# Attention scores on half of TensorE's rows per head, two units at a time, with q and k turned by one DMA

## The chip, the cores and the metric

The kernel runs on one core of a Trainium2 chip. The metric is the device time of one execution in microseconds. A run is called slow only if it is over 1.5% above the fastest run of the same kernel; every time compared here is of fast runs unless a sentence says otherwise. Five engines work beside each other: TensorE (PE, with its weight loads PEld), VectorE (DVE), ScalarE (ACT), GpSimd (POOL) and SyncE (SP), which here issues DMA.

## The reference, cut to what matters

```python
# q, k, v: [4 batches, 8 heads, 768 tokens, 64]; is_retrieval = [1,0,1,0,0,0,1,0]
scores = q @ k.T / sqrt(64)
keep   = causal if retrieval head else causal & (key < 4 or q - key < 64)
a      = softmax(where(keep, scores, -1e9))
x      = (a @ v) -> [3072 tokens, 512]
h      = x @ w_in                     # [3072, 2048]
out    = (h - tanh(h)) @ w_out        # [3072, 512]
```

## The kernel before

The 3072 tokens are cut into 12 tiles of 256 tokens (NG = 3 to a batch, NB = 2 blocks of 128 tokens in each). The eight heads form four pairs; one pair in one tile is a *unit*. Tiles 0 to 2 treat all heads alike. From tile 3 on the heads are sorted by their retrieval flag ("ranked"), so that half of the units need only the keys near the query. A planner written into the kernel orders all instructions beforehand; it lays score units, attention-value products (`av`), the first dense layer (`ph`) and the second (`po`) between each other on TensorE.

A head has only 64 elements, and the array has 128 rows. The kernel before fills all rows all the same: a 128-row tile of q holds both heads of a pair, and k of each head is stored with the other head's 64 rows set to zero.

```python
GROUPS = {                      # (key block, first query block, query blocks)
    0: [[(0, 0, 2), (1, 1, 1)]],
    1: [[(2, 0, 2), (3, 1, 1), (1, 0, 1)], [(1, 1, 1), (0, 0, 2)]],
    2: [[(4, 0, 2), (5, 1, 1), (3, 0, 1)], [(3, 1, 1), (0, 0, 2)], [(1, 0, 2), (2, 0, 2)]],
}
def st_S(n, gi):                # one group of one unit
    ...
        for hh in range(2):     # head 0 first, then head 1
            o = 0
            for jb, q0, nb in grp:
                nc.tensor.matmul(
                    out=sc()[:, hh, o : o + nb * 128],
                    lhsT=kk[:, hh, jb * KS : jb * KS + 128],           # 128 rows, 64 of them zeros
                    rhs=q_of(t, hp)[:, q0 * 128 : (q0 + nb) * 128], ...)
                o += nb * 128
    ...   # exp on ScalarE into pt, mask on VectorE
```

Ranked tiles are gathered, cast to fp16 on GpSimd one head at a time, and turned by SyncE's DMA transposes, q and k apart:

```python
def cast_ranked(t):
    ...                                         # zero the padding of k once per buffer
    for half in range(2):
        for nm in "kqv":
            for rank in range(half * HH, half * HH + HH):
                ...  # nc.gpsimd.tensor_copy(out=..., in_=r()[:, :, at, :])   24 casts a tile
    for nm in "kq":
        for i in range(NB):                     # 4 transposes a tile
            ...
                if nm == "k": o, src = kz[b % 2][:, :, c0 : c0 + 128], kp          # 8 blocks
                else:         o, src = qT[t]()[:, :, i * 128 : ...], t16s["q", t]() # 4 blocks
                nc.sync.dma_start_transpose(out=o, in_=src[:, i, :, :]...)
```

The softmax here doesn't subtract the row's maximum and nothing guards it: scores larger than these inputs give would overflow.

## Time and profile before

| | before |
|---|---|
| time, median of 3 runs | 250.95 us (250.09 to 251.23) |
| span of the profiled run | 249.8 us |
| PE / DVE / ACT / POOL busy | 231.0 / 147.0 / 146.9 / 100.5 us |
| score matmuls | 412, with 70,656 columns |
| DMA packets | 120,133 |

The first part of the page gives the busy time of each engine, its share of the span, and its instructions:

```profile
PE 231.0 (92%) x2220; PEld 176.1 (70%) x2220; DVE 147.0 (59%) x363; ACT 146.9 (59%) x225; POOL 100.5 (40%) x288
```

PE is far ahead of the others. But a busy share is an average over a start in which PE waits for loads, a weak stretch between 50 and 77 us, and a long stretch in which it never rests; the prediction takes them apart. One more view is SyncE's timeline (start, length, engine, line, operation) around the first ranked tile:

```profile
60.25 2.73 SPq L714 DMA_TRANSPOSE kz<-k  x2
63.16 2.50 SPq L714 DMA_TRANSPOSE qT<-t_q  x2
```

The reader is to see two transposes of k, with 8 blocks of 128 columns each, and two of q, with half as many blocks. The first ranked scores come in PE's timeline after the last of them:

```profile
68.30 0.49 PE L1000 MATMUL sc<-qT,kz 128*128 128x256 f16 x4
```

### The profile page before, as it was taken

Reading aid. Unit: us, or ns where it says so; the run is one execution under the profiler, and the core shown is the slowest. Engines: PE = TensorE matmul, PEld = TensorE weight load, DVE = VectorE, ACT = ScalarE, POOL = GpSimd, SP = SyncE. Lnnn points to the kernel's source line nnn. Section 1 sums busy time; section 2 is a strip of 40 time slices with the busy share of each in tenths; the row PEclk is TensorE's granted clock in tenths of the full one; section 3 lists DMA queues with packets and bytes.
Section 4 is the critical chain, followed back from the end, with each engine's and each line's share of the span. In section 5 each row is a group of like instructions: output and inputs, shape, how many; then the busy total and the mean of one; then the engine's idle time right before and its main releaser. Section 6 shows DMA issues by size and latency. Waiting matters only on the chain. (4 is left out here: it accounts for less than half of the span.)

```text
span 249.8 us, 6122 instructions
## 1 busy us (share of the span) xinstructions
PE 231.0 (92%) x2220; PEld 176.1 (70%) x2220; DVE 147.0 (59%) x363; ACT 146.9 (59%) x225; POOL 100.5 (40%) x288
## 2 busy tenths in 40 slices
PE   1788989989969999999999999999999999999992
PEld 0466978757657689877777777777877777777751
DVE  7555854495397486857946655467676554643410
ACT  3578855487462677864567575647567566443330
POOL 5386260009997443946716359265340000000000
PEclk9999999999988999999999999999999999999997
DMA  6999999996799899959979999999962211031111
GB/s 137 220 189 206 214 211 133 206 219 115 172 242 148 178 162 201 187 128 267 192 181 194 172 228 179 228 185 174 217 133 87 59 42 43 3 87 45 42 69 63
DMA packets 120133, 38.47 MB, mean 154 GB/s; under 512 B 114338, under 2 KB 116642, under 8 KB 120098
## 3 DMA queue, kind: packets, MB, share of 16 engines
q1 hardware_dynamic: 110882, 32.91, 67.4%
q0 software_dynamic: 8928, 4.98, 14.4%
q8 instruction: 18, 0.29, 0.5%
q10 hardware_dynamic: 288, 0.14, 0.2%
q14 instruction: 17, 0.14, 0.2%
HBM read 27.27 MB, written 6.29 MB: 134 GB/s over the span
## 5 line engine op out<-in xcount | busy, mean ns | idle before, releaser
L1172 PE MATMUL ph<-xT,win 128*128 128x256 f16 x768 | 101.1, 274 | 1.0 <-DVE gt L1192 0.8
L1231 PE MATMUL po<-wout,gt 128*128 128x512 f16 (+1 forms) x400 | 98.7, 373 | 0.3 <-ACT ot L1207 0.2
L1192 DVE SCALAR_TENSOR_TENSOR gt<-th,ph 128x512 f16<-128x512 f32 x96 | 65.6, 684 | 49.9 <-ACT th L1185 49.8
L1185 ACT ACTIVATE th<-ph 128x512 f32<-128x512 f32 x96 | 57.3, 599 | 60.1 <-PE ph L1172 58.5
L1172 PEld LDWEIGHTS <-win 128*128 128x128 f16 x768 | 81.2, 114 | 10.6 <-issue 1.9
L1018 ACT ACTIVATE pt<-sc 128x768 f16<-128x768 f32 (+1 forms) x60 | 54.0, 917 | 12.4 <-PE sc L1000 12.1
L1231 PEld LDWEIGHTS <-gt 128*128 128x128 f16 x400 | 37.3, 98 | 24.1 <-DVE gt L1192 0.8
L697 POOL CAST k<-raw_k 128x128 f16 x72 | 19.7, 309 | 45.5 <-DMA raw_k<-in_k_dram 27.6
L1067 PEld LDWEIGHTS <-pt 128*128 128x128 f16 x552 | 26.2, 98 | 11.7 <-DVE pt L1031 2.3
L1000 PE MATMUL sc<-qT,kz 128*128 128x256 f16 (+1 forms) x280 | 32.8, 251 | 1.3 <-DMA qT<-t_q 0.7
L1000 PEld LDWEIGHTS <-kz 128*128 128x128 f16 x280 | 23.3, 99 | 9.2 <-issue 2.2
L1067 PE MATMUL av<-v,pt 128*128 128x65 f16 x304 | 25.7, 195 | 2.0 <-DVE pt L1031 2.0
L697 POOL CAST v<-raw_v 128x128 f16 x72 | 21.7, 341 | 9.1 <-DMA raw_v<-in_v_dram 9.1
L697 POOL CAST t_q<-raw_q 128x128 f16 x72 | 21.7, 330 | 7.0 <-DMA raw_q<-in_q_dram 6.6
L1097 DVE TENSOR_TENSOR x16t<-av,rinv 128x128 f32 x72 | 20.8, 289 | 2.0
L1067 PE MATMUL av<-vf,pt 128*128 128x65 f16 x248 | 20.4, 193 | 1.4 <-ACT pt L1018 0.9
L1207 ACT ACTIVATE ot<-po 128x512 f32<-128x512 f32 (+1 forms) x24 | 14.2, 590 | 12.0 <-PE po L1231 9.6
L943 ACT ACTIVATE pt<-sc 128x1024 f16<-128x1024 f32 (+1 forms) x18 | 17.2, 955 | 6.0 <-PE sc L929 4.6
L1087 DVE RECIPROCAL rinv<-av 128x4 f32<-128x4 f32 x48 | 8.6, 179 | 13.9 <-PE av L1067 13.4
L1036 DVE TENSOR_TENSOR pt<-pt,m 128x1024 f16<-128x1024 f16 x16 | 11.8, 735 | 8.3 <-ACT pt L1018 8.2
L960 DVE TENSOR_TENSOR pt<-pt,mS 128x512 f16<-128x512 f16 x24 | 10.0, 456 | 7.3 <-ACT pt L943 7.3
L929 PE MATMUL sc<-qT,kz 128*128 128x128 f16 x132 | 10.4, 220 | 0.0
(73 smaller groups left out, 127.2 us busy)
## 6 DMA issues: line engine op xcount, KB each, us to landing
out_dram<-ot SPq DMA_DIRECT2D x23, 256.0 KB, 2.4
raw_q<-in_q_dram SPq DMA_DIRECT2D x18, 256.0 KB, 4.8
raw_k<-in_k_dram SPq DMA_DIRECT2D x18, 256.0 KB, 4.4
raw_v<-in_v_dram SPq DMA_DIRECT2D x18, 256.0 KB, 4.6
win<-in_moe_w_in_dram POOLq DMA_DIRECT2D x4, 512.0 KB, 8.8
wout<-in_moe_w_out_dram POOLq DMA_DIRECT2D x4, 512.0 KB, 15.9
raw_q<-in_q_dram SPq DMA_DIRECT2D x8, 128.0 KB, 3.8
raw_k<-in_k_dram SPq DMA_DIRECT2D x8, 128.0 KB, 3.8
```

What stands on the lines that cost most here:

```text
L697: nc.gpsimd.tensor_copy(out=o, in_=r()[:, :, at, :])
L943: lambda: nc.scalar.activation(out=pt()[:, :, 0:wid], in_=sc()[:, :, 0:wid], func=AF.Exp, scale=inv_sqrt_d),
L1000: nc.tensor.matmul(out=sc()[:, hh, o : o + nb * 128], lhsT=kk[:, hh, jb * KS : jb * KS + 128], rhs=q_of(t, hp)[:, q0 * 128 : (q0 + nb) * 128],
L1018: lambda: nc.scalar.activation(out=pt()[:, :, 512 * gi : 512 * gi + wid], in_=sc()[:, :, 0:wid], func=AF.Exp, scale=inv_sqrt_d,),
L1036: nc.vector.tensor_mul(out=pv, in0=pv, in1=m4[:, hs, 256:512].unsqueeze(2).to_broadcast([128, 2, 2, 256]),)
L1067: nc.tensor.matmul(out=av()[:, i, hh, :], lhsT=pt()[:, hh, co : co + 128], rhs=vv, start=(jb == first_jb), stop=(jb == qb),)
L1097: nc.vector.tensor_mul(out=x16s[t]()[:, :, at, :], in0=av()[:, :, hh : hh + 1, 0:D], in1=rinv()[:, :, hh : hh + 1].unsqueeze(3).to_broadca ...
L1172: nc.tensor.matmul(out=ph()[:, j, :], lhsT=w()[:, cb, c0 + fb % 4 : c0 + 512 : 4], rhs=xTs[t]()[:, cb, :], start=(cb == 0), stop=(cb == HP ...
L1185: lambda: nc.scalar.activation(out=th()[:], in_=ph()[:], func=AF.Tanh, scale=1.0 / XS),
L1192: lambda: nc.vector.scalar_tensor_tensor(out=gts[t]()[:, u * FU : (u + 1) * FU, :], in0=th()[:], scalar=-XS, in1=ph()[:], op0=ALU.mult, op ...
L1207: nc.scalar.activation(out=ot()[:, c0:c1], in_=po()[:, c0:c1], func=AF.Copy, scale=1.0 / XS)
L1231: nc.tensor.matmul(out=po()[:, c0:c1], lhsT=gts[t]()[:, f, ts * 128 : ts * 128 + 128], rhs=w_out_t[f // 4]()[:, f % 4, c0:c1], start=(f == ...
```

## The change

The intent is to let the two heads of a pair work at the same time, one on rows 0 to 63 and one on rows 64 to 127 of the array. Then no zeros are needed. Score groups of two units are put behind each other, so that TensorE changes between 128-row and 64-row work less often. And since k is no longer wider than q, both lie in one tile, are cast in one instruction per head, and are turned in one transpose per block.

```diff
-    kz = [const.tile([128, H, 2 * NG * KS], FP16, name=f"kz{s}") for s in range(2)]
-    k16 = [const.tile([128, NB, H, 128], FP16, name=f"k16_{x}") for x in range(2)]
+    qk = [const.tile([128, 2 * HP, 2 * NG, KS], FP16, name=f"qk{s}") for s in range(2)]
+    t16 = [const.tile([128, NB, 2, H, D], FP16, name=f"t16_{x}") for x in range(2)]
 ... (zero_kz and its eight calls go, and so does the memset of k16)
-                for nm in "kqv":
+                for nm in ("qk", "v"):
 ...
+                                nc.gpsimd.tensor_copy(
+                                    out=t16[t % 2][:, :, :, rank : rank + 1, :],
+                                    in_=raws["rqk", t][0]()[:, :, :, at, :],
+                                )
 ...
-            for nm in "kq":
-                for i in range(NB):
 ...
+            for i in range(NB):
+                def turn(i=i):
+                    nc.sync.dma_start_transpose(
+                        out=qk[b % 2][:, :, g * NB + i, 0:128],
+                        in_=t16[t % 2][:, i].rearrange("p x h d -> p (x h d)"),
+                    )
 ...
-        def st_S(n, gi):
+        def st_S(*units):
 ...
+                for n, gi, grp, wid, sc, key, added in todo:
+                    for jb, c0, i, nb in grp:
+                        for hh in range(2):
+                            p_ = slice(64 * hh, 64 * hh + 64)
+                            nc.tensor.matmul(
+                                out=sc()[:, hh, o : o + nb * 128]...,
+                                lhsT=ks...[p_, jb * KS + c0 : jb * KS + c0 + 128],
+                                rhs=qs[p_, q0 + i : q0 + i + nb, 0:128], ...
+                            )
 ...
+            two = 1 if todo[0][0] // HP in (0,) else 2
+            clusters.setdefault(todo[0][0], []).append(todo[:two])
```

## The prediction

> **What bounds the kernel now.** I began with the table of stretches (busy time of each engine, granted clock, DMA share), cut where the character of the run changes.
>
> ```profile
> 0.00:23.00 23.00, 14.20 (x125) 9.16 (x126) 14.50 (x52) 14.46 (x25) 13.88 (x31) 1.00 1.10 186
> 23.00:50.00 27.00, 26.15 (x252) 21.73 (x251) 14.94 (x32) 16.24 (x30) 6.93 (x8) 1.00 1.28 192
> 50.00:77.00 27.00, 23.56 (x257) 16.82 (x255) 18.45 (x54) 17.92 (x26) 20.23 (x59) 0.94 0.97 183
> 77.00:245.00 168.00, 166.97 (x1596) 128.35 (x1592) 98.71 (x226) 98.26 (x146) 59.50 (x190) 1.00 0.72 142
> 245.00:250.00 5.00, 0.15 (x2) 0.00 (x0) 0.42 (x1) 0.00 (x0) 0.00 (x0) 0.73 0.13 40
> ```
>
> The columns are the length, then PE, PEld, DVE, ACT and POOL busy, then clock, DMA share and GB/s. From 77 to 245 us PE is busy 166.97 of 168 us, and no other engine is above 98.71: TensorE is the bound there, and in 23 to 50 us (26.15 of 27). Two stretches are different. Before 23 us PE works 14.20 us and waits for first loads and casts. In 50 to 77 us it stands 3.4 us, and the clock drops. The page's groups say what the scores cost:
>
> ```profile
> L1018 ACT ACTIVATE pt<-sc 128x768 f16<-128x768 f32 (+1 forms) x60 | 54.0, 917 | 12.4 <-PE sc L1000 12.1
> L697 POOL CAST k<-raw_k 128x128 f16 x72 | 19.7, 309 | 45.5 <-DMA raw_k<-in_k_dram 27.6
> ...
> L1000 PE MATMUL sc<-qT,kz 128*128 128x256 f16 (+1 forms) x280 | 32.8, 251 | 1.3 <-DMA qT<-t_q 0.7
> ...
> L929 PE MATMUL sc<-qT,kz 128*128 128x128 f16 x132 | 10.4, 220 | 0.0
> ```
>
> The busy time of a matmul includes its tail, which lies beside the next one, so I take the pace from starts in PE's timeline:
>
> ```profile
> 48.04 0.94 PE L1000 MATMUL sc<-qT,kz 128*128 128x256 f16 x10
> 48.81 0.60 PE L1172 MATMUL ph<-xT,win 128*128 128x256 f16 x4
> ...
> 70.20 0.60 PE L1172 MATMUL ph<-xT,win 128*128 128x256 f16 x4
> 72.82 0.36 PE L1067 MATMUL av<-v,pt 128*128 128x65 f16 x6 [2.02 <-DVE pt L1031]
> 73.02 0.61 PE L929 MATMUL sc<-qT,kz 128*128 128x128 f16 x6
> 73.42 1.06 PE L1231 MATMUL po<-wout,gt 128*128 128x512 f16 x2
> ```
>
> Ten score matmuls hold 1792 columns (1024 of one group, 768 of the other) and take 48.81 - 48.04 = 0.77 us: 0.43 ns a column. The kernel has 140 score matmuls of 256 columns and 272 of 128: 70,656 columns, 30.4 us of PE's stream. Half of the rows of each are multiplied by zeros. The last lines show the hole: 2.02 us of waiting, then two 512-column matmuls in 0.86 us (73.42 to the next start, 74.28) where 0.43 is usual, thus at half clock. DVE's timeline has its origin:
>
> ```profile
> 69.73 3.03 DVE L1031 TENSOR_TENSOR pt<-pt,m 128x768 f16<-128x768 f16 x1 [0.35 <-ACT pt L1018]
> 72.68 0.64 DVE L953 TENSOR_TENSOR pt<-pt,mS 128x768 f16<-128x768 f16 x1
> 73.25 0.68 DVE L1192 SCALAR_TENSOR_TENSOR gt<-th,ph 128x512 f16<-128x512 f32 x1
> 73.84 0.17 DVE L1087 RECIPROCAL rinv<-av 128x4 f32<-128x4 f32 x1
> 73.94 0.54 DVE L1031 TENSOR_TENSOR pt<-pt,m 128x768 f16<-128x768 f16 x1
> ```
>
> The same mask takes 3.03 us once and 0.54 us four microseconds later; meanwhile POOL runs casts without a pause.
>
> **What the Trainium skill says.** (1) "TensorEngine Tiling (Array Packing)", Key Properties: tiles run independently, but changing the mode drains TensorE; its Gotcha 1 wants different row tiles in different PSUM banks. No matmul before uses fewer than 128 rows, so this trace can neither agree nor disagree; the diff does put the two heads in separate 512-float halves. (2) "TensorE: Matmul & The Clock Gate", Part 3: tiles of different rows overlap, four of 32 rows gave 3.07 times; Part 2 puts the drain of the array at about 128 cycles, 53 ns at 2.4 GHz. Here a lone tail can be read: a 128-column matmul is busy 220 ns and streams 128 x 0.43 = 55, so 165 ns of latency follow it. (3) The same page, Part 1: after an idle window the clock halves for about 3.4 us. The trace agrees: half pace from about 73 to 77 us after the 2.02 us hole. (4) "GPSIMD Engine Reference", Key points: GpSimd shares SBUF interfaces with VectorE, contending with two-input VectorE instructions. The 3.03 us mask agrees.
>
> **The change part by part.** The order of the built kernel shows the same 412 score matmuls, each on 64 rows, heads alternating, in 41 unbroken runs (before: 69): four single units in the first tile, then 37 pairs of groups. The other PE counts are unchanged.
>
> *Scores.* If two heads truly overlap, 30.4 us become 15.2. What lies before 23 us is worth little, since PE waits there anyway: 6,656 columns and 6 runs. After 23 us there remain 64,000 columns, 27.5 us, half of which is 13.8 us saved. A 128-column pair needs two weight loads in 55 ns; 65-column matmuls start every 30 ns with a load each, so two loads are about 60 ns. This lengthens the 136 such pairs by some 5 ns, 0.7 us; I leave it inside the next figure.
>
> *Mode changes.* 35 runs after 23 us mean 70 changes. The floor is the 53 ns of (2). The ceiling is the whole 165 ns tail and then a bare weight load (98 ns on the page), 263 ns. In between, the array drains and one load is laid bare: 53 + 98 = 151 ns, less whatever overlaps. I choose 125 ns: 70 x 0.125 = 8.8 us. That the author pairs units at all says that a change isn't free. Net on the path: 13.8 - 8.8 = **5.0 us**.
>
> *First ranked tile (50 to 77 us).* POOL now casts q and k of a head in one instruction: 216 casts become 144, of which 72 have twice the size. From 0.31 us for 128 elements and 0.62 for 512, one of 256 is estimated at 0.41, so 72 x (0.41 + 0.34) = 54 us in place of 63; the zero memsets of k (2 x 0.52 us) go and the sink copies halve. Per tile, all q and k casts end about 1.7 us earlier, and the transposes, four issues from 60.25 to 65.66 us in SyncE's timeline, become two, 8 blocks of 128 columns in place of 12. The first ranked scores can thus start some 2 to 3 us sooner. The hole costs 2.0 us and the half clock half of 3.4, 1.7: 3.7 us. Whether a mask meets a train of casts again is chance, so I count 60%: **2.2 us**.
>
> *Start.* VectorE loses the eight zero memsets (1.02 to 4.28 us) and half of the k copies (30 to 18 in all, 0.29 us each). The first score waited 0.45 us for a k copy; after that the loads rule: **0.3 us**.
>
> *Cost.* A pair fills both score buffers at once, so it waits for both earlier exponentials, and two follow in a row on ACT (0.8 to 1.0 us each), ahead of a tanh that frees a hidden-layer bank. ACT is at 59% and PE has other matmuls to run, so I put down only **0.8 us** of new waits.
>
> *Beside the path.* DMA moves a third fewer transpose blocks, DVE 3.0 + 3.5 us less, POOL some 12 us less. From 77 us on none of that is what PE waits for: worth nothing by itself.
>
> Sum: 250.95 - 5.0 - 2.2 - 0.3 + 0.8 = **244.25 us**.
>
> **Rivals.** *Changes cost the ceiling.* 70 x 0.263 = 18.4 us against 13.8: PE loses 4.6, and the time is 250.95 + 4.6 - 1.7 = 254. For it speaks the 165 ns tail; against it that the array's own part of the tail is only a third and that the change was built around few runs. *Changes are nearly free.* At the floor they cost 3.7 us, PE gains 10.1, and the time is about 239. For it: PE pulls weight loads ahead, which hides them everywhere in this trace. *The two heads don't overlap* (the same feeding path, or loads that serialise): the 13.8 us vanish and some 8.8 are added: 258 or so. Only the skill's 3.07 of four speaks against it. *Another bound takes over.* In 23 to 50 us the DMA share is 1.28 and POOL waits 27.6 us for k; a faster PE asks for data sooner. But from 77 us on the share is 0.72, transposes shrink, and SyncE loads two tiles ahead. If the pairing stalls PE more than I think (2 to 3 us), the time ends at 246 to 247.
>
> **Range and chances.** The cost of a change dominates: every 25 ns move the end by 1.75 us. 75 to 180 ns spans 240.7 to 248.1; the hole adds about 2 us either way. I give 238.5 to 249.5. The limit of 2% is 245.9; my centre is 1.7 us below it, about half of my spread: faster by over 2% with 0.62, within 2% with 0.31, slower by over 2% with 0.07.
>
> **What would show it.** In the changed profile, starts of the two matmuls of a head pair should lie within some 10 ns, and a run of 1792 columns should last about 0.385 us plus two changes. From the last 128-row start to the first 64-row start beyond the stream's own time I expect 100 to 150 ns, and the same on the way back. PE should still be about 99% busy from 77 us to some 238. The hole near 70 us should be smaller and the half clock gone or short. If the starts don't pair, the halving is wrong; if gaps exceed 190 ns, the cost of changes is; if PE shows waits for exponentials or score buffers over 1 us in all after 77 us, pairing has become a bound of its own; waits for the transposed q and k there would mean that DMA has.

## The result, and the profile after

The changed kernel took 241.63 us (median of 4 runs, 240.8 to 243.5), the kernel before 251.09 us in the same rounds (250.09 to 252.69). A ratio in this document is the mean time of one kernel's fast runs over that of the other's of the same rounds, so it is not quite the ratio of the medians quoted. Here it is 0.963, with a 95% interval of 0.955 to 0.970. The profiled run of the changed kernel, with a span of 239.1 us, was the fastest of its four; a second trace of the same kernel, taken later as a control, has 241.3 us.

The first part of the page after, and the table of stretches (length; PE, PEld, DVE, ACT, POOL busy; clock; DMA share; GB/s), cut at the same times:

```profile
PE 221.2 (93%) x2220; PEld 158.0 (66%) x2220; DVE 138.3 (58%) x343; ACT 144.8 (61%) x225; POOL 87.6 (37%) x214
```

```profile
0.00:23.00 23.00, 14.16 (x137) 8.86 (x138) 11.20 (x40) 14.94 (x26) 13.92 (x31) 1.00 1.10 187
23.00:50.00 27.00, 25.25 (x253) 19.34 (x251) 15.53 (x41) 17.45 (x31) 6.44 (x7) 1.00 1.35 202
50.00:77.00 27.00, 25.43 (x323) 17.62 (x322) 18.13 (x55) 19.83 (x29) 18.87 (x49) 1.00 0.95 210
77.00:234.00 157.00, 156.08 (x1513) 112.10 (x1512) 93.01 (x210) 92.61 (x141) 48.33 (x128) 1.00 0.63 130
```

PE is still the bound in the long stretch (156.08 of 157 us), and that stretch is some 11 us shorter. Between 50 and 77 us PE is busier (25.43 us in place of 23.56), does 323 matmuls where it did 257, and the clock no longer drops. Between 23 and 50 us it is a little less busy than before. The groups of the page that answer to those of before:

```profile
L906 ACT ACTIVATE pt<-sc 128x1024 f16<-128x1024 f32 (+1 forms) x78 | 68.2, 925 | 9.3 <-PE sc L886 8.1
L630 POOL CAST t<-raw_rqk 128x256 f16 x72 | 27.7, 427 | 58.8 <-DMA raw_rqk<-in_k_dram 42.6
...
L886 PE MATMUL sc<-qk 64*128 64x128 f16 (+1 forms) x412 | 23.0, 239 | 1.5 <-DVE qk L776 1.2
L886 PEld LDWEIGHTS <-qk 64*128 64x128 f16 x412 | 13.7, 95 | 12.6 <-issue 8.9
```

All 412 score matmuls are `64*128` now. The cast of q and k together took 427 ns (the prediction put 410). The pace is read from starts, as before:

```profile
119.62 1.03 PE L1139 MATMUL po<-wout,gt 128*128 128x512 f16 x4
120.58 0.62 PE L886 MATMUL sc<-qk 64*128 64x128 f16 x14
121.13 0.20 PE L975 MATMUL av<-vf,pt 128*128 128x65 f16 x1
...
123.31 1.04 PE L1080 MATMUL ph<-xT,win 128*128 128x256 f16 x8
124.28 0.56 PE L886 MATMUL sc<-qk 64*128 64x128 f16 x12
124.77 1.04 PE L1139 MATMUL po<-wout,gt 128*128 128x512 f16 x4
```

The 14 matmuls of the first run hold 2048 columns and last 121.13 - 120.58 = 0.55 us. On 128 rows at 0.43 ns a column they would have taken 0.88. The cost of the change is in the same lines: eight `ph` matmuls of 256 columns stream for 0.87 us, but the next start comes after 0.97 (124.28 - 123.31). Those 0.1 us are the way into the 64-row mode.

I took the whole trace apart in this way. The *stream* is each matmul's columns at 2.4 columns a nanosecond (0.417 ns each) plus 2.5 ns (fitted to the starts of back-to-back matmuls in these traces, which lie 56 ns apart for 128 columns, 109 for 256 and 216 for 512), halved where two heads work as a pair. A *change* is what lies beyond the stream at the edges of a 64-row run (counted up to 0.10 us going in and 0.11 going out). *Waits* are all the rest of the time between two starts, half clock included. From first to last start of a matmul, in us:

| kernel | stream | changes | waits to 23 us | 23-50 | 50-77 | after 77 | sum |
|---|---|---|---|---|---|---|---|
| before | 220.5 | 0 | 9.2 | 1.0 | 6.1 | 2.5 | 239.3 |
| after | 205.3 | 8.3 | 7.5 | 2.8 | 2.4 | 2.2 | 228.5 |
| after, second trace | 205.3 | 8.3 | 8.6 | 2.6 | 2.4 | 3.6 | 230.7 |

So 15.2 us of stream went, 8.3 came back as changes, and waits fell by 3.9 us in the one trace and by 1.6 in the other. The median of a change over the runs is 95 ns going in and 106 ns coming out. The two starts of a head pair lie 3 to 4 ns apart.

The hole near 70 us has gone. VectorE's timeline shows the mask of the first ranked tile:

```profile
64.64 0.73 DVE L936 TENSOR_TENSOR pt<-pt,m 128x768 f16<-128x768 f16 x1
65.29 0.75 DVE L924 TENSOR_TENSOR pt<-pt,mS 128x768 f16<-128x768 f16 x1
...
66.27 0.56 DVE L936 TENSOR_TENSOR pt<-pt,m 128x768 f16<-128x768 f16 x1
```

It takes 0.73 us, where the same mask took 3.03 before, although GpSimd casts the next tile beside it here too (62.84 to 66.30 us). Its scores start earlier (62.76 us, before 68.30), and so does what they rest on. First GpSimd's first casts of q and k before, then those after, then SyncE's transposes and PE's first ranked scores after:

```profile
55.88 0.29 POOL L697 CAST k<-raw_k 128x128 f16 x1 [17.91 <-DVE pt L1036]
```

```profile
53.66 2.48 POOL L630 CAST t<-raw_rqk 128x256 f16 x7 [16.03 <-DVE qk L776]
```

```profile
56.75 2.75 SPq L648 DMA_TRANSPOSE qk<-t  x2
```

```profile
62.76 0.51 PE L886 MATMUL sc<-qk 64*128 64x256 f16 x10
```

The casts start 2.2 us earlier. The transposes are through at 59.50 us (56.75 + 2.75), where the four of before were through at 65.66 (63.16 + 2.50).

### The profile page after: what moved, and what is told of

It is laid out like the page before. It is cut to its first block, busy times and chain, and to the rows that moved or that the text cites. A ratio compares the mean times of both kernels' runs of the same rounds, so it can differ in the third digit from the quotient of the medians.

```text
span 239.1 us, 5924 instructions
## 1 busy us (share of the span) xinstructions
PE 221.2 (93%) x2220; PEld 158.0 (66%) x2220; DVE 138.3 (58%) x343; ACT 144.8 (61%) x225; POOL 87.6 (37%) x214
## 5 line engine op out<-in xcount | busy, mean ns | idle before, releaser
L1080 PEld LDWEIGHTS <-win 128*128 128x128 f16 x768 | 80.0, 114 | 14.1 <-issue 3.0
L906 ACT ACTIVATE pt<-sc 128x1024 f16<-128x1024 f32 (+1 forms) x78 | 68.2, 925 | 9.3 <-PE sc L886 8.1
L630 POOL CAST t<-raw_rqk 128x256 f16 x72 | 27.7, 427 | 58.8 <-DMA raw_rqk<-in_k_dram 42.6
L625 POOL CAST v<-raw_rv 128x128 f16 x72 | 22.5, 353 | 6.1 <-DMA raw_rv<-in_v_dram 6.1
L886 PE MATMUL sc<-qk 64*128 64x128 f16 (+1 forms) x412 | 23.0, 239 | 1.5 <-DVE qk L776 1.2
L886 PEld LDWEIGHTS <-qk 64*128 64x128 f16 x412 | 13.7, 95 | 12.6 <-issue 8.9
L931 DVE TENSOR_TENSOR pt<-pt,mS 128x512 f16<-128x512 f16 x24 | 11.1, 503 | 6.6 <-ACT pt L906 6.6
L793 PEld LDWEIGHTS <-t 128*128 128x128 f16 x48 | 4.2, 109 | 9.2 <-ACT t L594 5.7
L701 POOL TENSOR_TENSOR vf<-v,rflagr 128x260 f16<-128x260 f16 x12 | 7.3, 615 | 0.0
L471 DVE TENSOR_SCALAR m<-A,thr 128x512 f16<-128x512 f16 x16 | 5.9, 418 | 2.0 <-PE sc L873 1.6
```

What stands on the lines that cost most here:

```text
L625: nc.gpsimd.tensor_copy(out=v1s[b]()[:, lo : lo + NB, rank : rank + 1, 0:D], in_=raw_of("v", t)[:, :, at, :],)
L630: nc.gpsimd.tensor_copy(out=t16[t % 2][:, :, :, rank : rank + 1, :], in_=raws["rqk", t][0]()[:, :, :, at, :],)
L886: nc.tensor.matmul(out=sc()[:, hh, o : o + nb * 128].rearrange("p (i c) -> p i c", c=128), lhsT=ks.rearrange("p i c -> p (i c)")[p_, jb * ...
L906: lambda pt=pt, gi=gi, wid=wid, sc=sc: nc.scalar.activation(out=pt()[:, :, 512 * gi : 512 * gi + wid], in_=sc()[:, :, 0:wid], func=AF.Exp, ...
L1080: nc.tensor.matmul(out=ph()[:, j, :], lhsT=w()[:, cb, c0 + fb % 4 : c0 + 512 : 4], rhs=xTs[t]()[:, cb, :], start=(cb == 0), stop=(cb == HP ...
```

## The experiments

Three theories stood after the result. *Rows*: the gain is the two heads at once, less what the changes of mode cost. *Hole*: a good part is that the first ranked tile comes sooner, for which casts, transposes or zeros could be the reason. *Pairing*: the order of matmuls inside a run, or the pairing of units, matters by itself. Eleven kernels were run. All passed the comparison with the reference; two of them (e4, e8) compute wrong scores, and pass all the same, probably because q and k of standard deviation 0.1 make scores so small that the softmax hardly feels them. The kernel before took 251.83 us (e1 to e4) and 252.5 on another chip. So the ratios are compared, not the times.

### e1: one unit at a time

```diff
-            two = 1 if todo[0][0] // HP in (0,) else 2
+            two = 1
```

> The changed kernel with every score unit alone: 70 runs of half-row matmuls in place of 41, nothing else. Theory (a run costs some 0.2 us of mode changes, 0.095 in and 0.106 out as in the changed kernel's trace, and all of it is on the path): 29 x 0.2 = 5.8 us more, 247.4 us. Rival 1 (pairing stalls PE on the score buffers, singles are smoother): 240 us or less. Rival 2 (a change is hidden, pairing is worth nothing): 241 to 242 us.

It took 248.14 us, ratio 0.985 (0.980 to 0.990). With 70 runs of scores in place of 41 the changes sum to 14.2 us in place of 8.3. That is 5.9 us more, and the time is 248.14 us against 243.16 in the control, 5.0 us apart (by the ratios, 0.985 against 0.965 and 0.963, it is 4.9 to 5.5 us). Up to 1.7 us of this may be something else: all four runs of e1 show a granted clock of 0.988 to 0.991, and in its trace the clock is halved from 21.3 to 24.7 us, which neither trace of the changed kernel shows. A change costs the same as in the paired kernel (96 ns and 106 ns). In PE's timeline a run of eight matmuls takes 0.33 us (125.23 - 124.90), of which 0.11 is the way out; the way in, another 0.1, lies before its start (the eight `ph` stream for 0.87 us and take 0.97):

```profile
123.93 1.04 PE L1080 MATMUL ph<-xT,win 128*128 128x256 f16 x8
124.90 0.40 PE L886 MATMUL sc<-qk 64*128 64x128 f16 x8
125.23 1.04 PE L1139 MATMUL po<-wout,gt 128*128 128x512 f16 x4
```

Changes are thus on the path, and their number is what pairing units is for.

### e2: head 0's matmuls first, then head 1's

```diff
-                    o = 0
-                    for jb, c0, i, nb in grp:
-                        for hh in range(2):
-                            p_ = slice(64 * hh, 64 * hh + 64)
+                    for hh in range(2):
+                        p_ = slice(64 * hh, 64 * hh + 64)
+                        o = 0
+                        for jb, c0, i, nb in grp:
```

> The changed kernel with the loops swapped: in each group first all matmuls of head 0, then all of head 1, so that neighbours use the same rows and can't overlap except at a seam. Mode changes stay at 41 runs. Theory (the gain comes from two row tiles streaming at once): the score stream goes back from 15.2 to nearly 30.4 us, of which 13.6 lie after 23 us, less a seam of some 0.1 us for each of 78 groups: +6 to +13 us, 248 to 255 us. Rival (PE looks ahead and overlaps them anyway, or the gain has another source): 241 to 243 us.

The loss that I expected did not come: 242.9 us, ratio 0.967 (0.961 to 0.973), the same as the changed kernel.

```profile
120.83 1.03 PE L1139 MATMUL po<-wout,gt 128*128 128x512 f16 x4
121.78 0.63 PE L886 MATMUL sc<-qk 64*128 64x128 f16 x14
122.34 0.20 PE L975 MATMUL av<-vf,pt 128*128 128x65 f16 x1
```

The run of 14 matmuls (2048 columns) takes 0.56 us although in the program all of head 0's matmuls of a group stand before head 1's. One after the other they would need 2048 x 0.417 = 0.85 us for the stream alone. The single starts in the trace show how. The second group of this run is, in program order, 256, 128, 128 columns of head 0 and then 256, 128, 128 of head 1; by start it is

```
122.019 (256 columns)  122.032 (256)  122.128 (128)  122.141 (128)  122.184 (128)  122.197 (128)
```

The second 256-column matmul, head 1's first, starts 13 ns after the first and ahead of two matmuls that precede it in the program. (In the built program, PE's instructions stand in the program's order, so it was not the compiler that moved them.) TensorE thus finds the other head's work by itself, within the two or three matmuls that stood between here. Alternating the heads in the program is not what earns the time.

### e3: the kernel before, with half rows alone

```diff
-                for hh in range(2):
-                    o = 0
-                    for jb, q0, nb in grp:
+                o = 0
+                for jb, q0, nb in grp:
+                    for hh in range(2):
+                        p_ = slice(64 * hh, 64 * hh + 64)
-                            lhsT=kk[:, hh, jb * KS : jb * KS + 128],
-                            rhs=q_of(t, hp)[:, q0 * 128 : (q0 + nb) * 128],
+                            lhsT=kk[p_, hh, jb * KS : jb * KS + 128],
+                            rhs=q_of(t, hp)[p_, q0 * 128 : (q0 + nb) * 128],
 ... (the same for the near units, and the planner's cost of a score group set to fit)
```

> The kernel before, with zeros, separate transposes and its own order, but each score matmul on its head's 64 rows and the heads alternating: 69 runs. Theory: 13.6 us of stream saved after 23 us, some 60 runs there x 0.2 us = 12 us given back: about 1.5 us faster than before, 249.5 us, if the hole near 70 us stays as it is (246 if it closes). Rival (the halving alone makes the whole gain): 241 to 242 us.

It took 251.52 us, ratio 0.9995 (0.994 to 1.005): no gain at all. The stream is shorter by the same 15.2 us, but the 69 runs of the old order cost 14.0 us of changes. The little that is left, 1.2 us, is lost in waits. The table of waits has PE wait for DMA, in us in total, times, and the longest:

```profile
PE sc L1003 <- DMA qT<-t_q: 2.9, 4, 0.9
...
PE ph L1175 <- DMA xT<-x16t: 1.3, 2, 1.0
```

Before, the first of these was 0.7 us and the second absent. After 77 us the waits are 7.1 us, before 2.5. So halving the rows pays here only with fewer runs. The waits for SyncE's queue can't come from a faster PE here, since stream and changes together are only 1.2 us shorter than before. PE comes earlier all the same, because the hole near 70 us is missing (waits up to 77 us are 13.2 us, before 16.3), although this kernel has the casts, the transposes and the zeros of before. Its first ranked mask runs in the middle of a train of casts, and takes 0.64 us:

```profile
69.15 0.64 DVE L1034 TENSOR_TENSOR pt<-pt,m 128x768 f16<-128x768 f16 x1 [0.30 <-ACT pt L1021]
69.33 1.48 POOL L697 CAST v<-raw_v 128x128 f16 x3
```

### e4: the changed kernel on all rows

```diff
-                            p_ = slice(64 * hh, 64 * hh + 64)
+                            p_ = slice(0, 128)
 ... (and the planner's cost of a score group set to that of before)
```

The result is wrong: both heads' products are added in each head's scores.

> The changed kernel with all 128 rows in each score matmul (so that the two heads' scores are added: a wrong result on purpose), no mode changes, everything else of the change kept. Theory: 13.6 us of stream come back after 23 us and 7.1 us of mode changes go: +6.5 us, 248.1 us, which leaves some 3 us of the gain to the other parts (the hole near 70 us). Rival (the other parts are worth nothing): 251 us, as before.

It took 246.82 us, ratio 0.981 (0.976 to 0.987). So everything but the rows is worth 251.83 - 246.82 = 5.0 us; I had put 3 here, and 2.5 less the cost of pairing in the prediction. The rest of the ratio, from 0.981 to the changed kernel's 0.965 or 0.963, is what the rows are worth net of their changes: 4.0 to 4.6 us, where the prediction had 5.0. Stream and changes together are 6.9 us shorter (15.2 - 8.3), so more than 2 us of that were met by new waits. The stream is that of before (220.5 us) and there are no changes of mode; waits are 13.2 us in place of 18.8. The half clock is gone, and the waits between 50 and 77 us fall from 6.1 to 1.6 us. The table of stretches shows this at full rows and with 25.92 us of busy PE:

```profile
50.00:77.00 27.00, 25.92 (x303) 19.84 (x301) 17.17 (x57) 19.17 (x28) 17.45 (x45) 1.00 0.92 206
```

### e5: the kernel before, with one tile's casts held back

The casts of tile 4 wait for a value of the first ranked tile's exponentials, so that GpSimd is idle while VectorE masks.

```diff
+                held = op("POOL", 100,
+                    lambda: nc.gpsimd.tensor_copy(out=gate2[:], in_=pts[n]()[0:1, 0, 0:1]), ...)
-                            port=True,
+                            port=True, after=held,
 ... (a memset of k is held too, and the casts of tile 4 are planned one unit later)
```

> The kernel before with one edit: GpSimd's casts for tile 4 wait (by a one-element copy that reads the masked tile) until the first two masks of tile 3 are done. Theory (the hole near 70 us is a mask held up by GpSimd's train of casts, and the half clock follows from it): the mask takes 0.55 us in place of 3.03, the 2.0 us wait and the half clock go, about 3 us faster than before, 248 us. Rival (the hole has another cause, such as too little work for PE there): 250 to 252 us with the wait still there under another name.

```profile
69.97 0.56 DVE L1040 TENSOR_TENSOR pt<-pt,m 128x768 f16<-128x768 f16 x1 [0.35 <-ACT pt L1027]
```

The mask that took 3.03 us takes 0.56 without casts beside it, and the waits between 50 and 77 us fall from 6.1 to 3.2 us. That fits the theory, but it doesn't settle it. Casts beside a mask are not enough to stretch it so: the same mask beside casts took 0.64 us in e3 and 0.73 in the changed kernel. In the thirteen kept traces some 200 masks have casts beside them for more than 0.7 of their time, and after the 3.03 us the longest took 0.92. So the 3.03 us is a rare event in the one trace that was kept of the kernel before; what sets it off stays open.

The half clock behind it was not usual either. It lasts 3.4 us, which takes 0.007 from the mean granted clock of a run of 250 us (the profiled run has 0.988). Of 19 runs of the kernel before, 14 have 0.996 or more and so can't have had it, and they are no faster (250.76 to 254.32 us) than the other five (251.26 to 253.07). The hole is thus a poor measure of what the change could gain.

As a test of what the hole is worth the run failed: it took 254.67 us, ratio 1.009 (1.005 to 1.012). The held casts run from 71.4 to 80 us in place of 66.7 to 75, the transposes behind them come late, and waits after 77 us rise to 7.8 us, part of it a half clock of 3.4 us from 97.7.

### e6 and e9: q and k turned apart again

e6 put two transposes into each planned step, but let the planner count one:

```diff
-                    nc.sync.dma_start_transpose(
-                        out=qk[b % 2][:, :, g * NB + i, 0:128],
-                        in_=t16[t % 2][:, i].rearrange("p x h d -> p (x h d)"),
-                    )
+                    for x in range(2):
+                        nc.sync.dma_start_transpose(
+                            out=qk[b % 2][:, x * HP : (x + 1) * HP, g * NB + i, 0:128],
+                            in_=t16[t % 2][:, i, x].rearrange("p h d -> p (h d)"),
+                        )
```

> The changed kernel with two crossbar transposes for a block, one for q and one for k, in place of one: same data, 18 more issues. Theory (not on the path; the queue of SyncE has room): within 0.5 us of the changed kernel, 241 to 242.2 us. Rival (the transposes pace the ranked tiles): 2 us or more slower, 243.5 us or above, with PE waiting on transposes.

It took 257.92 us, ratio 1.022 (1.017 to 1.026), 16 us above what I expected. Its table of waits has one line with three stands of up to 4.5 us, and its clock was halved four times (at 18.3, 76.3, 120.7 and 178.7 us):

```profile
PE ph L1081 <- DMA xT<-x16t: 9.4, 3, 4.5
```

The planner had counted too little for SyncE, so the size says nothing fair about the change. e9 therefore gives each transpose a planned step of its own and its own key:

```diff
-                op(
-                    "SP", 1250, turn, ...
-                    w=[("qk", b % 2, "all", g, i)], dma=(1024, 22.0),
-                )
+                for x, nm in ((1, "k"), (0, "q")):
+                    ...
+                    op(
+                        "SP", 1250, turn, ...
+                        w=[("qk", b % 2, nm + "all", g, i)], dma=(512, 22.0),
+                    )
```

> The changed kernel with separate transposes for q and k again, this time as operations of their own, so that the planner counts each issue on SyncE's queue (in the earlier run it counted one for two). Theory A (each transpose holds SyncE's queue some 1.3 us whatever its size; with PE faster the queue paces the ranked tiles): still 4 us or more slower than the changed kernel, above 246 us, PE waiting on the transposes of x and of q and k. Theory B (the earlier loss came from the planner's false count alone): 241 to 243.5 us.

It took 248.6 us, the median of its three fast runs (245.85 to 249.33; the fourth, 249.84, counts as slow), ratio 0.981 (0.974 to 0.989). The changed kernel's ratio in the same rounds was 0.965, so about 1.6% of the time, some 4 us, is lost by this alone. SyncE's timeline shows why:

```profile
57.25 5.63 SPq L650 DMA_TRANSPOSE qk<-t  x4
68.01 6.99 SPq L650 DMA_TRANSPOSE qk<-t  x4
```

Four transposes of 4 blocks each hold the queue for 5.6 to 7.0 us, where two of 8 blocks took 2.75 for the same bytes. What the queue is charged for is the transpose, not its size: the median of all is 1.30 us with 8 blocks (changed kernel) and 1.27 with 4 (e9). PE then waits for q and k, and for the turned x of the dense layer, which goes through the same queue:

```profile
PE sc L888 <- DMA qk<-t: 3.8, 3, 1.6
PE ph L1082 <- DMA xT<-x16t: 2.0, 1, 2.0
```

A half clock of 3.4 us follows the stand of 2.0 us. In the first trace of the changed kernel there is 0.9 us for x (2.3 in the second) and none for q and k:

```profile
PE ph L1080 <- DMA xT<-x16t: 0.9, 1, 0.9
```

### e7: the zeros put back

Eight memsets of the old size go into a tile that nobody reads, at the place where the old ones stood.

```diff
+            for c0, c1 in ((0, TT), (TT, S)):
+                for hp in range(HP):
+                    op("DVE", (c1 - c0) * 1.06 + 20,
+                        lambda hp=hp, c0=c0, c1=c1: nc.vector.memset(spare[:]..., 0.0), w=["spare"])
```

> The changed kernel with the eight zero memsets of the kernel before put back at the start of VectorE's work, on a tile that nobody reads. Theory (the loads rule the start; what the zeros cost is the 0.3 us of the prediction): 241.6 to 242.2 us. Rival (VectorE's 3.3 us stood on the path to the first scores): 243.5 to 245 us.

It took 243.42 us, the median of its five fast runs (241.86 to 245.31; the sixth, 245.61, counts as slow), ratio 0.966 (0.961 to 0.971). The changed kernel has 0.965 in its five-round control. The zeros at the start cost nothing that can be measured here.

### The control: the changed kernel again

> The changed kernel unedited, as the control of this group: a ratio of 0.963 to the kernel before, 241 to 243 us.

It took 243.16 us (242.38 to 245.06), ratio 0.965 (0.961 to 0.969). In its trace one wait for the turned x at 113 us takes 1.6 us, which the first trace does not have. That is the larger part of the difference between the two traces.

### e8: both heads on the same 64 rows

```diff
-                            p_ = slice(64 * hh, 64 * hh + 64)
+                            p_ = slice(0, 64)
 ... (and the planner's cost set to fit)
```

The result is wrong: head 1's scores are head 0's. All else, the 64-row mode, the runs and the transposes, is that of the changed kernel; only the second row half is not used.

> The changed kernel with both heads of a pair on the same 64 rows (rows 0 to 63; a wrong result on purpose): the same 41 runs and mode changes, but no second row tile that could run beside the first. It replaces the loop swap, which showed that PE pairs the tiles whatever their order. Theory (the whole gain of the scores is two row tiles at once): the score stream goes back to 30.4 us, 13.6 us more after 23 us, and the mode changes stay: 241.6 + 13.6 = 255 us, slower than the kernel before. Rival (64-row matmuls are cheaper in themselves, or the gain lies elsewhere): 242 to 248 us.

It took 255.17 us, ratio 1.011 (1.006 to 1.016), which is 12.0 us above the control. A run of 1792 columns took 0.49 us in the changed kernel (124.77 - 124.28 above, in twelve matmuls); here it takes 124.76 - 123.89 = 0.87 us, in ten:

```profile
123.89 0.94 PE L886 MATMUL sc<-qk 64*128 64x256 f16 x10
124.76 0.24 PE L975 MATMUL av<-v,pt 128*128 128x65 f16 x2
```

That is the whole stream of 1792 x 0.417 = 0.75 us, with the way out and the fixed 2.5 ns a matmul. A matmul on 64 rows is no faster than one on 128. What halves the time is that two of them, on different rows, run together. (Its clock was halved once for 3.4 us, near 21.5 us, where PE waits for loads anyway.)

### e10: q and k cast apart, but turned together

```diff
-                for nm in ("qk", "v"):
+                for nm in "kqv":
 ...
-                                    out=t16[t % 2][:, :, :, rank : rank + 1, :],
-                                    in_=raws["rqk", t][0]()[:, :, :, at, :],
+                                    out=t16[t % 2][:, :, "qk".index(nm), rank : rank + 1, :],
+                                    in_=raw_of(nm, t)[:, :, at, :],
```

> The changed kernel with q and k cast separately again (216 casts on GpSimd in place of 144), the single transpose kept. Theory (what closed the hole near 70 us is that q and k of the first ranked tile are cast 5 us sooner, partly by the merged casts): the first ranked scores start 1 to 3 us later, 242 to 245 us, perhaps with a hole again. Rival (casts don't matter): 241 to 242.5 us and first ranked scores where they were, near 62.8 us.

It took 242.4 us, ratio 0.963 (0.958 to 0.969), the same as the control. SyncE's timeline and PE's first ranked scores:

```profile
59.72 2.75 SPq L648 DMA_TRANSPOSE qk<-t  x2
```

```profile
64.55 0.51 PE L886 MATMUL sc<-qk 64*128 64x256 f16 x10
```

The single casts delay the transposes by 3.0 us (59.72, after 56.75), to nearly the moment of before (60.25). The first ranked scores still start at 64.55 us, 3.8 us sooner than before. The transposes are over at 62.47 us, before at 65.66. (In e9, with four transposes but merged casts, they are over at 62.88, and the first ranked scores start at 64.13.) No hole opens. The merged casts are worth nothing here; the merged transposes are.

The traces of these kernels, taken apart as above:

| kernel | stream | changes | waits to 23 us | 23-50 | 50-77 | after 77 | sum |
|---|---|---|---|---|---|---|---|
| e1 singles | 205.3 | 14.2 | 9.2 | 3.4 | 2.3 | 2.6 | 237.0 |
| e3 before, half rows | 205.3 | 14.0 | 8.7 | 1.0 | 3.5 | 7.1 | 239.5 |
| e4 after, all rows | 220.5 | 0 | 7.7 | 2.3 | 1.6 | 1.6 | 233.7 |
| e9 turned apart | 205.3 | 8.4 | 8.3 | 2.6 | 3.5 | 8.1 | 236.1 |
| e10 cast apart | 205.3 | 8.3 | 7.9 | 2.5 | 2.4 | 3.0 | 229.4 |

## Why the prediction was right or wrong

The predicted 244.25 us stands against 241.63 at first and 243.16 in the control; both lie in the range, and faster by over 2% was the likeliest of the three outcomes. The prediction was too slow by 1 to 2.6 us. That it came so near is in part luck: it left out a part of some 4 us ("Beside the path" below), and other terms were off the other way.

**The bound.** "TensorE is the bound there" was right, and it still is: 156.08 of 157 us.

**Scores.** "13.8 us saved" after 23 us was right: the stream lost 13.8 us there, and 15.2 in all. e8 shows that this gain is the two heads at once and nothing else. The second weight load, for which I put 5 ns a pair, cost nothing: 128-column pairs start 56 ns apart, as single matmuls did. The 1.4 us of stream in the first 23 us, which I left out, were met by 1.25 us of changes there, which I left out too.

**Mode changes.** The mechanism was right and the size was off. "I choose 125 ns: 70 x 0.125 = 8.8 us" measured 95 ns going in and 106 going out, thus 0.201 us a run and 35 x 0.201 = 7.0 us. The term was 1.8 us too large. e1 shows that the runs are on the path: 29 more of them added 5.9 us in the trace, and 4.9 to 5.5 us of time. Of the rivals, neither the ceiling of 263 ns nor the floor of 53 came true.

**First ranked tile.** The direction was right, the size too small and the reason partly wrong. "2.2 us" stands against 3.7 us in the waits between 50 and 77 us, the same in both traces. "The first ranked scores can thus start some 2 to 3 us sooner" measured 5.5 us (68.30 to 62.76). But I took the hole for a property of the kernel before, on one trace. Masks do meet trains of casts again, in the changed kernel too, and take 0.73 us; e3 has no hole with everything of before but the rows; and the half clock was absent in 14 of 19 runs of the kernel before. So the 3.7 us, and the closing of the hole, can't be put down to a part of the change, and how much of it is in the measured gain stays open. The earlier start of the scores is real: of its 5.5 us, 1.8 go again when the casts are apart (e10) and 1.4 when the transposes are (e9). How much of the rest is due to GpSimd's earlier start (53.66 in place of 55.88 us) stays open. One reading of the skill was too quick as well. "The trace agrees" holds for the 3.4 us of half clock, not for what set it off: Part 1 speaks of an idle window of some 3.4 us, and here a stand of 2.0 us was enough (in e9 too; one of 1.6 us, in the second trace of the changed kernel, was not).

**Start.** "0.3 us" for VectorE's zeros and copies: e7 finds nothing for the zeros. The waits before 23 us fell by 1.7 us in the first trace and by 0.6 in the second, so this cannot be told from the spread.

**Cost.** "Only 0.8 us of new waits" was put on exponentials and score buffers from pairing. After 77 us nothing of the sort shows (the longest such wait of PE in the whole trace sums to 1.2 us, in the first tiles). Between 23 and 50 us, however, waits rose by 1.8 us, and by 1.3 in e4, where rows are as before. So most of it comes with the new order, not with the faster scores. The table of waits of the changed kernel has two lines there that neither name nor time of before has:

```profile
PE tp7k L793 <- DVE gt L1100: 0.6, 1, 0.6
PE tp6q L793 <- DVE gt L1100: 0.4, 1, 0.4
```

They are TensorE's own transposes of q and k for the unranked tiles, which stand behind a VectorE instruction; e4 has both too, with 0.4 us each. The change moves these transposes to the front of a unit's slot where the next unit is paired with it, which may be why; no run tried it.

**Beside the path.** This is the step that failed: "From 77 us on none of that is what PE waits for: worth nothing by itself." It fits the trace of the kernel before (0.7 us of waits for DMA after 77 us), and I carried it over to one in which PE comes to the ranked tiles sooner. e3 and e9 show that without the merged transposes PE then waits for SyncE's queue: 7.1 and 8.1 us of waits after 77 us, 4.2 of them for DMA in each, where the changed kernel has 2.2 to 3.6, with 0.9 to 2.3 for DMA. I had counted blocks of DMA (8 in place of 12 a block of tokens), but the queue is charged for each transpose, and those went from four to two. The merged transpose gives some 4 us by e9; whether it gives as much with all rows, where e4 gains 5.0 us, no run tried. I had named it only in the first ranked tile, and as a rival ("another bound takes over") that I set aside because "SyncE loads two tiles ahead".

**The sum.** In the first trace the parts are -15.2 + 8.3 - 3.9 = -10.8 us from first to last start; the prediction had -13.8 + 8.8 - 2.2 - 0.3 + 0.8 = -6.7. Of the 4.1 us between them 1.4 are the stream before 23 us, 0.5 the changes (8.3 in all against 8.8 after 23 us) and 2.2 the waits. In the second trace, at -8.6 us, the waits fell by 1.6 us and my 1.7 for them would have been right. The rest of the kernel wanders by that much from run to run, most visibly in the wait for the turned x near 113 us.

## What to carry to other kernels

Two small-K matmuls on different rows of the array halve the stream, but each run of them costs about 0.2 us of changes: with 0.215 ns saved a column (half of 0.43), a run must hold more than 0.201 / 0.000215 = 935 columns to pay at all, so gather runs before halving rows. When an engine is made faster, count again what each other queue takes per step at the new pace: a side effect that was worth nothing before (here one transpose in place of two) can be what lets the gain through. Turn as much as possible in each transpose, since the queue's time went with their number, not their size.

## What the Trainium skill lacked or had wrong

- "TensorEngine Tiling (Array Packing)", Key Properties, says that changing the mode drains TensorE, without a number. Here it is 95 ns going into 64-row mode and 106 ns coming out, and nearly the same in every kernel that had it (medians 95 to 96 and 103 to 113 ns).
- "TensorE: Matmul & The Clock Gate", Part 3, The mechanism, says that matmuls keep strict program order in start and end. e2 contradicts this for starts on different row halves: a matmul of the other head started 13 ns after the first one and ahead of two that precede it in the program. Its 4 ns between the starts of packed tiles agree (3 to 4 ns in the changed kernel).
- "DMA: Bandwidth & Descriptors", DMA Transpose (X-bar), gives no time for a transpose on SyncE's queue (elsewhere the page has a bandwidth, and cycle counts in a comparison of chips). Here the median was 1.27 us with 4 blocks of 128 columns (e9) and 1.30 with 8 (changed kernel): two of 8 blocks 2.75 us, four of 4 blocks 5.63 us.
- "GPSIMD Engine Reference", Key points, names the contention with VectorE's two-input instructions without a size: here one mask took 3.03 us beside a train of casts and 0.56 us without it (e5), while some 200 others beside casts took at most 0.92.
